# Pairwise 64-row contractions, narrower q and k, and a searched TensorE order in a fused attention + FFN kernel

One core of a Trainium2 chip. The metric is device time in microseconds (us), the median of several runs; a profiled run also gives a span (first to last instruction), which is some 1.7 to 2.1 us shorter than the time.

## The reference, cut to what matters

```python
# S = 2048, D = 448, H = 16 heads of Dh = 28, FF = 1792; weights and x in bf16
xn = layernorm(x)
q, k, v = split(xn @ wqkv)                       # 3 x (S, H, 28)
pq, pk = q @ w_phi, k @ w_phi                    # per head, 28 x 28
phi_q = concat(softmax(pq), softmax(-pq))        # 56 features per head
phi_k = concat(softmax(pk), softmax(-pk))
kv  = phi_k^T @ v ;  z = sum_s phi_k             # per head
o   = (phi_q @ kv) / (phi_q @ z + 1e-6)
out = x + o.reshape(S, D) @ wo + silu(xn @ w1) @ w2
```

The contraction of all projections is 448 = 3.5 x 128. `w_phi` is folded into the q and k weights on the chip ("the fold"), which needs eight DMA transposes of `wqkv`.

Of the kernel before, what the change touches and what calls it, by code (L numbers as in the profile page):

```python
# [107 lines left out]
class _Op:  # L108
    __slots__ = ("id", "eng", "dur", "fn", "deps", "odeps", "table", "name", "start", "end",
                 "ticket", "sigreq", "is_dma", "xfer", "lat", "dma_sem", "dma_val", "users",  # L110
                 "out_slot", "prio", "slack")

    def __init__(self, id, eng, dur, fn, name, table=None):
        self.id = id
        self.eng = eng
        self.dur = dur
        self.fn = fn
        self.deps = set()
        self.odeps = set()
        self.table = table  # L120
        self.name = name
        self.start = None
        self.end = None
        self.ticket = None
        self.sigreq = False
        self.is_dma = False
        self.xfer = 0.0
        self.lat = 1700.0
        self.dma_sem = None
        self.dma_val = None  # L130
        self.users = []
        self.out_slot = None
        self.prio = 0
        self.slack = 0.0


class _Prog:
# [44 lines left out]
    def op(self, eng, dur, fn, reads=(), writes=(), keys_r=(), keys_w=(), table=None, name="",  # L182
           okeys_r=(), okeys_w=()):
        o = _Op(len(self.ops), eng, float(dur), fn, name, table)
        o.prio = self.cur_prio
        o.slack = self.cur_slack
# [17 lines left out]
    def dma(self, fn, xfer, reads=(), writes=(), name="", out_slot=None, eng="sp", issue=450.0, lat=1700.0):  # L204
        o = self.op(eng, issue, fn, reads, writes, name=name)
        o.is_dma = True
        o.xfer = xfer
        o.lat = lat
        o.out_slot = out_slot
        return o  # L210

    def schedule(self):
        ops = self.ops
        n = len(ops)
# [7 lines left out]
        def lat(d, o):  # L222
            if d.is_dma:
                return 0.0
            if d.eng == o.eng:
                return 0.0 if d.eng == "pe" else 60.0
            return 310.0 if d.eng == "act" else 200.0

        bl = [0.0] * n
        for o in reversed(ops):  # L230
            m = 0.0
            for u in o.users:
                uu = ops[u]
                m = max(m, lat(o, uu) + bl[u])
            extra = 2500.0 if o.is_dma else 0.0
            bl[o.id] = o.dur + extra + m
        self.bl = bl
# [6 lines left out]
        eng_free = {e: 0.0 for e in ENGINES}  # L244
        act_table = [None]
        dma_free = [0.0]
# [3 lines left out]
        FILL_TOL = 30.0  # L250

        def est(o):
# [6 lines left out]
            if o.eng == "act" and o.table is not None and act_table[0] is not None and o.table != act_table[0]:  # L259
                t += 1400.0  # L260
            return t

        while done < n:
            cands = []
            tmin = None
            for e in ENGINES:
                for oid in ready[e]:
                    o = ops[oid]
                    t = est(o)
                    cands.append((t, o))  # L270
                    if tmin is None or t < tmin:
                        tmin = t
            assert cands, "scheduler deadlock"
            best = None
            for t, o in cands:
                if t <= tmin + DELTA:
# [5 lines left out]
            for t2, o2 in cands:  # L282
# [8 lines left out]
            if o.is_dma:  # L291
                issue_end = t + o.dur
                xfer_start = max(issue_end, dma_free[0])
                xfer = o.xfer
                dma_free[0] = xfer_start + xfer
                o.end = xfer_start + xfer + o.lat
                eng_free[o.eng] = issue_end
            else:
                o.end = t + o.dur
                eng_free[o.eng] = o.end  # L300
                if o.eng == "act" and o.table is not None:
# [9 lines left out]
        return order  # L311


def bass_parallel_sum__linear_kernel_hedgehog__dense_activation_silu__prompt_kernel(
# [26 lines left out]


# [4 lines left out]
    with es:  # L347
# [13 lines left out]
        Wk = sb("Wk", [128, 4 * D], BF16)  # L361
        Wq_sb = sb("Wq", [128, 4, D], BF16)
        Wk_sb = Wk[:].rearrange("p (k c) -> p k c", k=4)
# [70 lines left out]
        def pe_mms(mms, name, dur=None, keys_w=()):  # L434
# [6 lines left out]
            for _, cnt in mms[0][2].ap[1:]:  # L441
                n *= cnt
            P.op("pe", dur if dur is not None else d_mm(n), fn, reads=[m[1] for m in mms] + [m[2] for m in mms],
                 writes=[m[0] for m in mms], keys_w=keys_w, name=name)
# [4 lines left out]
        def transposes(pairs, name):  # L449
# [5 lines left out]
            P.op("pe", 56.0 * len(pairs), fn, reads=[p[1] for p in pairs] + [ident[:]], writes=[p[0] for p in pairs], name=name)  # L455
# [33 lines left out]
        for i in range(38):  # L489
            P.op("pe", 107.0, lambda e: e.matmul(banks[3][:, 0:128], ones_bf[:], ones_bf[:], start=True, stop=True),  # L490
                 reads=[ones_bf[:]], writes=[banks[3][:, 0:128]], name="warm")
# [9 lines left out]
        def load_x(t0, t1):  # L501
            load(x_sb[:, t0:t1, :], xt[:, t0:t1, :], f"x{t0}")
# [12 lines left out]
        load_w1(0, 512, 3200.0)  # L515
        load_w1(512, 1024, 3200.0)
# [10 lines left out]
        def dma_t(dst, src, xfer, name, **kw):  # L527
            P.dma(lambda e: e.dma_start_transpose(out=dst, in_=src), xfer, lat=650.0, reads=[src] if kw.pop("sbuf", True) else [],
                  writes=[dst], name=name, issue=1250.0, **kw)
# [10 lines left out]
        def fold_loads():  # L540
            for a in range(8):
                dma_t(wT_sb[:, a, :], A_wqkv[:, a * KP:a * KP + 128], 600.0, f"wT_dma{a}", sbuf=False)

        def fold_mms():
            for kt, fb in enumerate((AUX, 2, AUX, 4)):
                for qk in range(2):
                    wps = banks[fb + qk][:, 0:G * KP].rearrange("p (g c) -> p g c", g=G)
                    P.cur_slack = 600.0
                    pe_mms([(wps[:, g, :], wT_sb[0:KP, qk * 4 + g, KS[kt]:KS[kt] + 128], BDphi[:, g, :], True, True) for g in range(G)],
                           "fold", dur=56.0 * G)  # L550
                    P.cur_slack = 0.0
                src = psum[:, fb * 512:(fb + 2) * 512].rearrange("p (b c) -> p b c", b=2)[:, :, 0:D]
                for qk, W in ((0, Wq_sb), (1, Wk_sb)):
                    if qk:
                        copy(W[:, kt, :], src[:, qk, :], 760, "fold_ev")
                    else:
                        act(W[:, kt, :], src[:, qk, :], ACTF.Identity, D, "fold_ev")


        def ln_tile(t):  # L560
# [26 lines left out]
            if t >= XN_DMA0:  # L587
                if t % 2:
                    dma_t(xnT[:, t - 1:t + 1, :, :].rearrange("p i k c -> p (i k) c"),
                          xn_sb[:, sl - 1:sl + 1, :].rearrange("p i c -> p (i c)"), 1300.0, f"xnT_dma{t}")  # L590
# [9 lines left out]

        def pair_block(b0, width, lhs, rhs, name):
            def fulls(st, c0=0, c1=width):
                for i in range(2):
                    for n, kt in enumerate((0, 1, 2 + i)):
                        part = () if (c0, c1) == (0, width) else (c0, c1)
                        mm(banks[b0 + i][:, c0:c1], lhs(i, kt, slice(0, 128)), rhs(i, kt, slice(0, 128), *part),
                           st and n == 0 and c0 == 0, not st and n == 2, name)

            def rem(st):
                rows = [slice(64, 128), slice(0, 64)]  # L610
                return [(banks[b0 + i][:, 0:width], lhs(i, 3 - i, rows[i]), rhs(i, 3 - i, rows[i]), st, not st) for i in range(2)]

            return fulls, rem

        def group(first, rest, name):
            for f in first:
                f[0](True)
            rems = []
            for f in first:
                rems += f[1](False)  # L620
            for f in rest:
                rems += f[1](True)
            pe_mms(rems, name, dur=216.0 * (len(first) + len(rest)) + 214.0)
            for f in first:
                f[2]()
            for f in rest:
                f[0](False)
                f[2]()

        def ffn1_block(fp, c, b0):  # L630
            tok = slice(c * 512, (c + 1) * 512)
            fulls, rem = pair_block(b0, 512, lambda i, kt, r: w1_sb[r, kt, (2 * fp + i) * 128:(2 * fp + i + 1) * 128],
# [6 lines left out]
            return fulls, rem, evac  # L639
# [3 lines left out]
        def v_block(t, b0):  # L643
            fulls, rem = pair_block(b0, D, lambda i, kt, r: xnT[r, t + i, kt, :],
                                    lambda i, kt, r: wv_sb[r, kt, :], "v")
# [6 lines left out]
            return fulls, rem, evac  # L652

        q_order = [14, 15, 4, 5, 6, 7, 0, 1, 8, 9, 2, 3, 10, 11, 12, 13]
# [4 lines left out]

        def proj_block(t, b0, is_k):  # L660
            W = Wk_sb if is_k else Wq_sb
            fulls, rem = pair_block(b0, D, lambda i, kt, r: xnT[r, t + i, kt, :],
                                    lambda i, kt, r: W[r, kt, :], "k" if is_k else "q")

            def evac():
                E2 = ek(t, 2)[:, :, 0:2 * D] if is_k else eq(t, 2)
                src = psum[:, b0 * 512:(b0 + 2) * 512].rearrange("p (i c) -> p i c", i=2)[:, :, 0:D].rearrange("p i (h f) -> p i h f", f=DH)
                dst = E2.rearrange("p i (h s f) -> p i h s f", s=2, f=DH)
                for sg in range(2):
                    act(dst[:, :, :, sg, :], src, ACTF.Exp, 896, "exp", scale=(1.0 if sg == 0 else -1.0), table="exp", okeys_w=["acttab"])  # L670
                E4 = E2.rearrange("p i (h f) -> p i h f", f=DH)
                R2 = Rec[:, int(is_k), t:t + 2, :]
                P.op("dve", 1985, lambda e: e.tensor_reduce(R2, E4, AXL.X, ALU.add), reads=[E4], writes=[R2], name="Ssum")  # L673
                P.op("dve", 555, lambda e: e.reciprocal(R2, R2), reads=[R2], writes=[R2], name="Rrec")  # L674

            return fulls, rem, evac
# [9 lines left out]
        def kv(t):  # L686
            def wide(c):
                return slice(0, 128) if c < CC - 1 else slice(0, KP)

            P.cur_slack = 500.0  # L690
            pe_mms([(banks[KVB][wide(c), c * 2 * DA:(c + 1) * 2 * DA], ek(t)[:, 0, c * KP:c * KP + wide(c).stop],
                     vaug[:, t, 2 * c:2 * c + 2, :].rearrange("p h c -> p (h c)"),
                     t == 0 and c == 0, t == NT - 1) for c in range(CC)], "kv_mm", dur=CC * 32.0, keys_w=["kvbank"])
# [28 lines left out]
        UB = 7  # L722
        ob_cnt = [0]

        def ffn2(t, bs, last):
            w = D // len(bs)
            for ft in range(FT):
                for n, b in enumerate(bs):
                    mm(banks[b][:, 0:w], hT[:, ft, t * 128:(t + 1) * 128], w2_sb[:, ft, n * w:(n + 1) * w],
                       ft == 0, last and ft == FT - 1, "ffn2_mm")  # L730

        def y_tile(t, b):
            P.cur_prio = 2
            ffn2(t, [b], True)
# [6 lines left out]
        u_cnt = [0]  # L741

        def att(t):
            n = u_cnt[0]
            q, uq, oq = n % NQ, n % NU, n % NO
            ub = banks[UB]
            u_cnt[0] += 1
            P.cur_slack = 600.0
# [282 lines left out]
```

## The kernel before: what the change touches

A small scheduler in the kernel lists operations with guessed durations and sets every engine's order. TensorE work comes in blocks of two 128-row output tiles in two PSUM banks: three full 128-row matmuls for each tile, and the half contraction of both as one pair of 64-row matmuls that run side by side in the array.

```python
def pair_block(b0, width, lhs, rhs, name):
    def fulls(st, c0=0, c1=width):
        for i in range(2):
            for n, kt in enumerate((0, 1, 2 + i)):
                mm(banks[b0 + i][:, c0:c1], lhs(i, kt, slice(0, 128)), ...)      # cut
    def rem(st):
        rows = [slice(64, 128), slice(0, 64)]
        return [(banks[b0 + i][:, 0:width], lhs(i, 3 - i, rows[i]), rhs(i, 3 - i, rows[i]), st, not st) for i in range(2)]

def group(first, rest, name):     # the 64-row pairs of 2 to 4 blocks stand together
    ...                           # cut: fulls of `first`, all pairs, fulls of `rest`

# SP's issue order after the loads: input transposes of tiles 4..7, then the weight transposes
chain([f"xnT_dma{t}" for t in (5, 7)] + [f"wT_dma{a}" for a in range(8)] + ["xnT_dma9", "w2"] + ...)
```

TensorE makes FFN1 blocks, v, k, q, the sums kv (58-wide matmuls), U = phi_q kv, and the output tiles. ScalarE empties PSUM (silu, exponentials, v), VectorE does layernorm, softmax sums and final additions, GpSimd scales phi_k and phi_q.

The softmax here doesn't subtract the row's maximum and nothing guards it: scores larger than these inputs give would overflow.

## Time and profile before

| | before |
|---|---|
| time, median of the first runs | 154.15 us (153.79 to 154.19) |
| span of the profiled run | 152.0 us |
| TensorE, first FFN1 matmul to last matmul's end | 6.62 to 149.41 = 142.79 us |
| changes between 128-row and 64-row matmuls | 40, 0.096 us each (median) |
| last matmul's end to end of span | 2.62 us |

The third and fourth lines come from the start times of single matmuls in the trace: the distance from one start to the next, less what the same width takes in an undisturbed run (216 ns for 512 columns, 189 for 448). A busy share alone would not show them. The lines of the profile are in the prediction below.

### The profile page before, as it was taken

Reading aid. Unit: us, or ns where it says so; the run is one execution under the profiler, and the core shown is the slowest. Engines: PE = TensorE matmul, PEld = TensorE weight load, DVE = VectorE, ACT = ScalarE, POOL = GpSimd, SP = SyncE. Lnnn points to the kernel's source line nnn. Section 1 sums busy time; section 2 is a strip of 40 time slices with the busy share of each in tenths; the row PEclk is TensorE's granted clock in tenths of the full one; section 3 lists DMA queues with packets and bytes.
Section 4 is the critical chain, followed back from the end, with each engine's and each line's share of the span. In section 5 each row is a group of like instructions: output and inputs, shape, how many; then the busy total and the mean of one; then the engine's idle time right before and its main releaser. Section 6 shows DMA issues by size and latency. Waiting matters only on the chain.

```text
span 152.0 us, 2799 instructions
## 1 busy us (share of the span) xinstructions
PE 147.6 (97%) x1118; PEld 78.4 (52%) x1118; DVE 89.6 (59%) x171; ACT 72.6 (48%) x86; POOL 67.4 (44%) x76
## 2 busy tenths in 40 slices
PE   7999999999999999999999999999999999999993
PEld 7794434354545555544444544445554555555482
DVE  1958897223048999897105312998953834284552
ACT  3557657393879857895555769774000000000000
POOL 7106455100017999999991000598998000000000
PEclk9999999999999999999999999999999999999999
DMA  4998644499940000000078310075899993534151
GB/s 96 339 370 311 126 89 94 86 237 273 245 129 4 0 0 2 6 0 0 4 138 172 64 40 4 0 136 104 164 118 206 210 195 61 67 102 120 37 157 65
DMA packets 44206, 17.38 MB, mean 114 GB/s; under 512 B 36640, under 2 KB 43808, under 8 KB 44192
## 3 DMA queue, kind: packets, MB, share of 16 engines
q1 hardware_dynamic: 41568, 15.44, 45.1%
q10 hardware_dynamic: 2624, 1.75, 3.9%
q8 instruction: 9, 0.15, 0.5%
q14 instruction: 5, 0.04, 0.1%
HBM read 6.56 MB, written 1.84 MB: 55 GB/s over the span
## 4 chain that ended last, share of the span: by engine, by line
PE 93%; ACT 3%; issue 1%; DVE 1%; POOL 0%; ACTq 0%; POOLq 0%
PE psum L438 90%; PE psum L490 3%; ACT Ek_sb L458 2%; PE psum L453 1%; ACT phT L458 1%; DVE Wk L462 0%; ACT xnT L458 0%; DVE x_sb L776 0%; POOL ones_bf L465 0%; ACTq L971 0%; POOLq L1016 0%
## 5 line engine op out<-in xcount | busy, mean ns | idle before, releaser
L438 PE MATMUL psum<-xnT,phT 128*128 128x512 bf16 (+2 forms) x278 | 48.3, 338 | 0.6 <-ACT xnT L458 0.3
L438 PE MATMUL psum<-w_sb,hT 128*128 128x448 bf16 (+1 forms) x238 | 48.5, 341 | 0.0
L458 ACT ACTIVATE hT<-psum 128x1024 bf16<-128x1024 f32 x28 | 28.1, 1025 | 19.4 <-PE psum L438 19.4
L706 POOL TENSOR_TENSOR RA<-Ek_sb,Rec 128x896 bf16<-128x896 bf16 x16 | 26.6, 1699 | 17.0 <-DVE Rec L674 17.0
L673 DVE TENSOR_REDUCE Rec<-Ek_sb 128x64 f32<-128x1792 bf16 x12 | 23.7, 1990 | 14.1 <-ACT Ek_sb L458 14.1
L438 PEld LDWEIGHTS psum<-w_sb,hT 128*128 128x128 bf16 x238 | 22.3, 98 | 17.5 <-issue 0.6
L438 PEld LDWEIGHTS psum<-xnT,phT 128*128 128x128 bf16 (+1 forms) x278 | 19.8, 98 | 21.6 <-issue 3.6
L458 ACT ACTIVATE Ek_sb<-psum 128x896 bf16<-128x896 f32 x24 | 20.4, 927 | 4.9 <-PE psum L438 3.2
L681 POOL TENSOR_TENSOR Ek_sb<-Ek_sb,Rec 128x896 bf16<-128x896 bf16 x8 | 13.3, 1698 | 4.5 <-ACT Ek_sb L458 4.4
L753 DVE TENSOR_SCALAR den<-psum 128x16 f32<-128x16 f32 x16 | 2.7, 172 | 20.6 <-PE psum L438 20.6
L438 PE MATMUL psum<-wv,xnT 128*128 128x448 bf16 (+1 forms) x64 | 13.4, 352 | 0.1
L438 PE MATMUL psum<-Wk,xnT 128*128 128x448 bf16 (+1 forms) x64 | 13.5, 354 | 0.0
L681 POOL TENSOR_TENSOR phT<-phT,Rec 128x896 bf16<-128x896 bf16 x8 | 13.3, 1698 | 0.0
L438 PE MATMUL psum<-Wq,xnT 128*128 128x448 bf16 (+1 forms) x64 | 12.5, 353 | 0.0
L563 DVE BATCH_NORM_STATS2 st<-x_sb 128x6 f32<-128x448 bf16 x16 | 9.6, 601 | 3.8 <-DMA x_sb<-in_A_x_dram 3.8
L438 PE MATMUL psum<-wo_sb,vaug 128*128 128x448 bf16 (+1 forms) x51 | 11.5, 341 | 0.0
L776 DVE TENSOR_TENSOR x_sb<-psum,x_sb 128x448 bf16<-128x448 f32 (+1 forms) x13 | 7.1, 583 | 6.2 <-PE psum L438 6.2
L578 DVE TENSOR_SCALAR RA<-x_sb,mv,rstd 128x384 bf16<-128x384 bf16 (+2 forms) x28 | 8.8, 349 | 2.7 <-POOL rstd L574 2.6
L760 DVE TENSOR_TENSOR vaug<-psum,rden 128x448 bf16<-128x448 f32 x16 | 9.9, 616 | 0.7 <-DVE rden L755 0.2
L674 DVE RECIPROCAL Rec<-Rec 128x64 f32<-128x64 f32 x16 | 8.6, 540 | 0.3
L673 DVE TENSOR_REDUCE Rec<-phT 128x64 f32<-128x1792 bf16 x4 | 8.0, 1990 | 0.6 <-ACT phT L458 0.6
L458 ACT ACTIVATE phT<-psum 128x896 bf16<-128x896 f32 x8 | 6.9, 930 | 2.9 <-PE psum L438 2.9
(49 smaller groups left out, 113.8 us busy)
## 6 DMA issues: line engine op xcount, KB each, us to landing
out_dram<-x_sb ACTq DMA_DIRECT2D x15, 112.0 KB, 2.4
w_sb<-in_B_w_dram SPq DMA_DIRECT2D x1, 1568.0 KB, 8.1
x_sb<-in_A_x_dram SPq DMA_DIRECT2D x3, 448.0 KB, 7.7
phT<-in_B_w_dram SPq DMA_DIRECT2D x2, 384.0 KB, 4.7
wo_sb<-in_A_wo_dram SPq DMA_DIRECT2D x2, 336.0 KB, 3.9
phT<-in_B_w_dram SPq DMA_DIRECT2D x1, 576.0 KB, 6.9
wv<-in_A_wqkv_dram SPq DMA_DIRECT2D x1, 336.0 KB, 7.3
phT<-in_B_w_dram SPq DMA_DIRECT2D x2, 128.0 KB, 4.6
```

What stands on the lines that cost most here:

```text
L438: r = e.matmul(dst, lhsT, rhs, start=st, stop=sp, skip_group_check=True)
L458: P.op("act", d_act(n), lambda e: e.activation(dst, src, func, scale=scale), reads=[src], writes=[dst], table=table, name=name, **keys)
L490: P.op("pe", 107.0, lambda e: e.matmul(banks[3][:, 0:128], ones_bf[:], ones_bf[:], start=True, stop=True), reads=[ones_bf[:]], writes=[ban ...
L563: P.op("dve", 590, lambda e: e.bn_stats(st6[:, t, :], xs), reads=[xs], writes=[st6[:, t, :]], name=f"bnst{t}", okeys_w=["ln"])
L578: P.op("dve", dur, lambda e: e.tensor_scalar(dst, x_sb[:, t, c0:c1], mv[:, t, 0:1], rstd[:, t:t + 1], ALU.subtract, ALU.mult), reads=[xs, ...
L673: P.op("dve", 1985, lambda e: e.tensor_reduce(R2, E4, AXL.X, ALU.add), reads=[E4], writes=[R2], name="Ssum")
L674: P.op("dve", 555, lambda e: e.reciprocal(R2, R2), reads=[R2], writes=[R2], name="Rrec")
L681: P.op("pool", 1700, lambda e: e.tensor_tensor(E3, E3, Rk[:, :, None].broadcast_to([128, 32, DH]), ALU.mult), reads=[E3, Rk], writes=[E3], ...
L706: P.op("pool", 1700, lambda e: e.tensor_tensor(dst, Eq, Rq.rearrange("p (c j) -> p c j", c=CC)[:, :, :, None].broadcast_to([128, CC, 4, DH ...
L753: P.op("dve", 190, lambda e: e.tensor_scalar(den[:, uq, :], U3[:, :, DH], EPS_DEN, None, ALU.add), reads=[U3[:, :, DH]], writes=[den[:, uq ...
L760: P.op("dve", 620, lambda e: e.tensor_tensor(o3, U3[:, :, 0:DH], rden[:, uq, :, None].broadcast_to([128, H, DH]), ALU.mult), reads=[U3[:, ...
L776: P.op("dve", d_dve(cs.stop - cs.start), lambda e: e.tensor_tensor(res[:, cs], ob, addend[:, cs], ALU.add), reads=[ob, addend[:, cs]], wri ...
```

## The change

Its intent: fewer mode changes, less matrix work, and no waits of TensorE. The core of the diff:

```diff
+            def half(i):            # i = 0 opens the block with 3 pairs, i = 1 closes it with 4
+                lo, hi = i, 1 - i
+                for n, (kl, kh) in enumerate(((0, 0), (1, 1), (2, 3)) if i == 0 else ((0, 0), (1, 1), (2, 2), (3, 3))):
+                    mms.append((banks[b0 + lo][:, 0:width], lhs(lo, kl, LOW), rhs(lo, kl, LOW), st, sp))
+                    mms.append((banks[b0 + hi][:, 0:width], lhs(hi, kh, HIGH), rhs(hi, kh, HIGH), st, sp))
+                ...                 # the closing half waits on TensorE's own semaphore for the opening half
-        Wk = sb("Wk", [128, 4 * D], BF16)                     # 448 columns
-        Wq_sb = sb("Wq", [128, 4, D], BF16)
+        Wqk = sb("Wqk", [128, 2, 4, DQ], BF16)                # DQ = 16 * 27 = 432
+        # the fold subtracts each head's last column from the other 27; the 28th exponential is a constant 1
+        P.op("dve", ..., tensor_tensor(dst, src, ref[...].broadcast_to([128, 2, H, DF]), ALU.subtract), name="fold_sub")
+PLAN = """aF3@4 aF4@0 bF3 aF5@2 av2@6 bF4 bv2 bF5 aF6@0 bF6 av0@4 bv0 aF7@0 aF8@2 aF10@4 bF8 bF10 bF7 f2@26 ...
+ ... W6 W1@2 W10 R3,6,13,1,5,10 F11@1:7 F11:6 F11:1 W11 r11"""    # a/b: open/close a block at a bank; f: fold
-        chain([f"xnT_dma{t}" for t in (5, 7)] + [f"wT_dma{a}" for a in range(8)] + ["xnT_dma9", "w2"] + ...)
+        chain("wT_dma0 wT_dma1 wT_dma2 wT_dma3 xnT_dma5 wT_dma4 xnT_dma7 wT_dma5 wT_dma6 wT_dma7 xnT_dma9 ... w2 ")
```

TensorE follows PLAN strictly; the other engines are still ordered by the scheduler, with new durations. In PLAN the sums kv (K), U and the output tiles (F, W, R) stand wherever the search put them, in any free bank.

## The prediction

> **What bounds the kernel now.** I read the page from the top: busy shares, slices, chain, groups; then the timeline of TensorE around its gaps, and the issue queue of SP. The page first:
>
> ```profile
> span 152.0 us, 2799 instructions
> PE 147.6 (97%) x1118; PEld 78.4 (52%) x1118; DVE 89.6 (59%) x171; ACT 72.6 (48%) x86; POOL 67.4 (44%) x76
> PE   7999999999999999999999999999999999999993
> PEclk9999999999999999999999999999999999999999
> PE 93%; ACT 3%; issue 1%; DVE 1%; POOL 0%; ACTq 0%; POOLq 0%
> L438 PE MATMUL psum<-Wk,xnT 128*128 128x448 bf16 (+1 forms) x64 | 13.5, 354 | 0.0
> ```
>
> TensorE is busy in every slice but the first and the last, at full clock, and is 93% of the chain. So only shorter or better packed TensorE work, or a shorter head or tail, can move the time. "Busy" hides waste, because matmuls overlap: a 448-wide one lasts 354 ns. So I took start-to-start distances of all matmuls instead. In runs of one kind they are constant: 216 ns for 512 columns, 189 for 448, 56 for 128, 29 for the 58-wide ones; two 64-row matmuls on opposite halves of the array start 3 to 5 ns apart, and such a pair takes as long as one full matmul. Everything above these numbers is waste.
>
> The largest waste is the change between 128-row and 64-row matmuls, here before and after the two pairs that end a set of output tiles:
>
> ```profile
> 116.45 0.73 PE L438 MATMUL psum<-wo_sb,vaug 128*128 128x448 bf16 x3
> 117.11 0.55 PE L438 MATMUL psum<-wor_sb,vaug 64*128 64x448 bf16 x4
> 117.59 0.40 PE L438 MATMUL psum<-KVm,phT 112*128 112x58 bf16 x8
> ```
>
> The third 128-row matmul starts at 116.45 + 2 x 0.189 = 116.83, so the first pair was due at 117.02 and starts at 117.11. The second pair starts at 117.31, so the next was due at 117.50 and starts at 117.59. Each change costs about 0.095 us, both ways. The trace has 20 such visits, so 40 changes: 3.8 us. The other gaps are few: 0.29 us at 19.5, 0.27 at 34.8 (a fold bank still being copied), 0.18 at 46.4, small ones early: about 0.9 us from the first projection matmul at 6.62 to the end. The first:
>
> ```profile
> 19.07 1.53 PE L438 MATMUL psum<-xnT,phT 128*128 128x512 bf16 x5
> 19.98 0.34 PEld L438 LDWEIGHTS psum<-xnT,phT 128*128 128x128 bf16 x3 [0.59 <-ACT hT L458]
> ```
>
> The named releaser is an activation, but the transposed input of tiles 6 and 7 landed at 19.87, so I put this wait down to that DMA.
>
> **What the Trainium skill says.** "TensorEngine Tiling (Array Packing)", Key Properties: changing the tiling mode drains TensorE, while tiles run independently; the trace agrees (0.095 us a change, pairs 4 ns apart). The same page, Gotcha 1: different row tiles cannot access one PSUM bank at the same time. The old kernel never tries, so no number here; it is why the new blocks come in two halves. "TensorE: Matmul & The Clock Gate", Back-to-back issue gap: N/2.4 + 2.5 ns warm; the trace agrees (216 at 512, 189 at 448), so 432 should take 182.5. "ScalarE: Activation LUTs", What ACT_TABLE_LOAD costs: about 1283 ns a load; the trace agrees (five of 1283 ns mean).
>
> **Part 1: 64-row contractions throughout.** A block makes two tiles of contraction 448 = 3.5 x 128. Before: six full matmuls and one 64-row pair. After: seven pairs (three opening, four closing, with banks swapped between the halves). The array time is the same, 7 x 216 = 1.51 us for an FFN1 block, 7 x 189 for v. Weight loads double in number, yet two 64-row loads are done within 0.10 us together in the trace, well under a pair's 0.19. What goes is the changes. Walking through the written order word by word (a block half or a remainder is 64-row, all else 128-row) I count 19 changes, plus the one after the head: 20 against 40. **Saved: 20 x 0.095 = 1.9 us**, all on TensorE.
>
> Price: a closing half writes with the lower rows where the upper rows of its opening half wrote, and it waits for TensorE's own semaphore. With another half between them (at least 0.55 us, against 0.38 for a matmul's end) this is free. Twice the order closes a block right after opening it (the seventh FFN1 block and the first v block): there a matmul's 0.38 us plus a semaphore's way stand against 0.22 or 0.19 due. **Added: about 2 x 0.22 = 0.45 us** (an estimate; no such wait is in the old trace).
>
> **Part 2: 432-wide q and k.** The last logit of each head is subtracted in the folded weights, so its exponential is 1. 16 tiles x 2 x 3.5 passes = 112 passes, each 16 columns shorter. 216 - 189 = 27 ns for 64 columns, so 6.7 ns a pass: **0.75 us saved**. 32 exponentials of 864 in place of 896 columns save ACT 0.03 us each. The fold gets two tiny ACT copies per bank pair and a wider DVE subtraction (about 1.05 us: the 0.62 of a 448-wide one plus 416 columns at some 1.04 ns); this matters only for when k can start.
>
> **Part 3: the order, and free placement of kv, U and output tiles.** It can remove at most the 0.9 us of old gaps. Matrix work itself is unchanged. Adding passes from the end of the head (first pair of block 3 at 12.04) at the spacings above, with the 19 changes and the two self-waits, the last matmul starts at 145.4, against 149.15. So with no wait at all TensorE ends 3.75 us earlier.
>
> I then checked, place by place, whether each bank's reader and each operand is ready, with durations of the old trace (silu every 0.91 us, exponentials 0.83, sums 1.99 + 0.54, scaling 1.67 per tile). **What I expect to wait:** (a) the fifth block needs bank 0 at 12.69; the first silu can start at 11.82 and takes 1.02: ready about 12.9, +0.2. (b) Four of the weight transposes now come before the input transposes:
>
> ```profile
> 6.90 0.92 SPq L499 DMA_DIRECT2D x_sb<-in_A_x_dram  x2
> 13.54 3.76 SPq L528 DMA_TRANSPOSE xnT<-RA  x2
> 17.34 11.23 SPq L528 DMA_TRANSPOSE Y_sb<-in_A_wqkv_dram  x8
> ```
>
> SP stood idle from 7.8 to 13.5, and the new order uses that; but those four queue behind input loads that land until 15.7. The second input transpose is then issued at about 18.6 instead of 16.05 and lands about 3.3 us later, near 21.9; TensorE wants it at about 21.4. +0.3, perhaps 0.7. (c) Many later places are within 0.2 us of each other (bank copies in the k/v stretch): +0.3 together. (d) Tail: the last tile is now a whole one: its eviction takes 0.62 instead of 0.39 us, and its store goes through the ACT queue after six others: +0.25.
>
> Sum: -1.9 - 0.75 - 0.9 + 0.45 + 0.2 + 0.3 + 0.3 + 0.25 = -2.05 us. 154.15 - 2.05 = 152.1; I say **152.0**.
>
> **The rivals.** *No waits:* if the search found an order that really keeps TensorE fed, only the tail is lost: -3.75 + 0.25 = -3.5, so 150.6. For it: the old kernel lost only 0.9 us to waits. Against: (a) follows from the trace directly. *GpSimd becomes the bound:* its scaling of k takes 16 x 1.67 = 26.7 us in a row. In the new order it can start near 43.1, so it ends at 69.8, and the last kv product stands at about 71.5 with my waits. A slip of 2 us there, or ones-column fills getting between, would hold TensorE 1 us or so: 153. Against: the slack; k starts some 13 us earlier than before. *The fold comes too early:* its products stand at 26.7 instead of 32.4 and need all eight weight transposes, the last of which lands, by the old latencies (2.6 to 3.9 us), between 25.1 and 26.4. A straggler costs 0.5 to 1 us: 152.5 to 153. *Pairs do not keep their pace over long runs:* the old trace has at most four in a row; 10 ns lost on each of some 310 pairs would be 3 us, and the time would be unchanged. Nothing in the trace suggests it.
>
> **Range and chances.** Better than 2% means under 151.1, so waits, self-waits and tail together must stay about 1 us below my sum; with three terms that I read off the trace I give it 0.22. Being slower by 2% needs over 6 us of new waits: 0.02. The no-wait case and the GpSimd, fold or transpose cases set the ends: 150.5 to 153.3.
>
> **What would show it.** TensorE: 20 changes of 0.09 us; long runs of pairs at 216, 189 and 183 ns; first matmuls of blocks unchanged until 12.0. Gaps of 0.2 at 12.7, of about 0.3 near 21.5, and two of 0.2 at the closing halves near 19 and 20.6. The last matmul should start near 146.5. The prediction is wrong if TensorE waits over 0.5 us before the last kv products, at the fold, or anywhere after 90 us, or if pairs run slower than full matmuls.

## The result

152.19 us (150.91 to 152.60, four runs) against 154.15: ratio 0.9867, 95% interval 0.9824 to 0.9911, 1.3% faster. Ratios here are the mean time of one kernel's fast runs over that of the other's of the same rounds, so not quite the ratio of the medians quoted. Results were correct in all runs, those of the experiments too.

Lines of the page of the changed kernel (the third is TensorE's busy share in 40 slices):

```profile
span 150.8 us, 3406 instructions
PE 144.0 (95%) x1412; PEld 79.1 (52%) x1412; DVE 91.4 (61%) x186; ACT 70.2 (47%) x86; POOL 70.9 (47%) x82
PE   7699968999999999999999999999999999999992
PE 93%; DMA 3%; issue 1%; SPq 1%; DVE 0%
L468 PE MATMUL psum<-Wqk,xnT 64*128 64x432 bf16 x224 | 22.9, 343 | 0.0
```

TensorE is again busy nearly everywhere, but the sixth slice (18.9 to 22.6 us) shows a 6. The chain of waits in order of time (start, us, what) says what the whole run looks like:

```profile
6.67 0.14 issue
6.80 1.21 PE psum L468 x18
...
12.88 0.04 issue
12.92 6.05 PE psum L468 x56
18.97 0.05 issue
19.02 1.62 PE psum L468 x14
20.64 0.05 issue
20.69 0.93 PE psum L468 x8
21.62 1.46 issue
23.08 124.98 PE psum L468 x1196
```

There are four interruptions: at 12.9, 19.0, 20.7 and 21.6 us. From 23.08 to 148.06 TensorE waits for nothing. The last interruption is the large one: 1.46 us without any matmul, and as a start-to-start distance 1.62 us more than due. SP's issue queue in the same run:

```profile
7.33 1.14 SPq L529 DMA_DIRECT2D x_sb<-in_A_x_dram  x2
8.51 7.71 SPq L558 DMA_TRANSPOSE Y_sb<-in_A_wqkv_dram  x4
16.26 1.31 SPq L558 DMA_TRANSPOSE xnT<-RA  x1
17.61 1.27 SPq L558 DMA_TRANSPOSE Y_sb<-in_A_wqkv_dram  x1
18.92 1.31 SPq L558 DMA_TRANSPOSE xnT<-RA  x1
```

The second input transpose (the last line) is issued at 18.92 and lands at 22.99; block 7, which needs tiles 4 to 7, starts at 23.08. In the kernel before, the two transposes of the input were issued at 13.54 and 16.05.

### The profile page after: what moved, and what is told of

Same layout as the page of the kernel before. It is cut to its first block, busy times and chain, and to the rows that moved or that the text cites. A ratio compares the mean times of both kernels' runs of the same rounds, so it can differ in the third digit from the quotient of the medians.

```text
span 150.8 us, 3406 instructions
## 1 busy us (share of the span) xinstructions
PE 144.0 (95%) x1412; PEld 79.1 (52%) x1412; DVE 91.4 (61%) x186; ACT 70.2 (47%) x86; POOL 70.9 (47%) x82
## 4 chain that ended last, share of the span: by engine, by line
PE 93%; DMA 3%; issue 1%; SPq 1%; DVE 0%
PE psum L468 92%; DMA phT<-in_B_w_dram 3%; SPq L529 1%; DVE x_sb L842 0%; PE psum L483 0%
## 5 line engine op out<-in xcount | busy, mean ns | idle before, releaser
L468 PE MATMUL psum<-xnT,phT 64*128 64x512 bf16 (+1 forms) x428 | 45.1, 350 | 2.2 <-issue 1.5
L468 PEld LDWEIGHTS psum<-xnT,phT 64*128 64x128 bf16 (+1 forms) x428 | 21.1, 95 | 22.7 <-issue 1.9
L728 DVE TENSOR_REDUCE Rec<-Ek_sb 128x32 f32<-128x896 bf16 (+1 forms) x20 | 24.3, 1246 | 13.7 <-ACT Ek_sb L488 7.9
L468 PEld LDWEIGHTS psum<-w_sb,hT 128*128 128x128 bf16 x238 | 21.6, 98 | 19.0 <-issue 1.5
L468 PE MATMUL psum<-Wqk,xnT 64*128 64x432 bf16 x224 | 22.9, 343 | 0.0
L488 ACT ACTIVATE Ek_sb<-psum 128x864 bf16<-128x864 f32 x24 | 20.3, 932 | 2.9 <-issue 2.6
L468 PEld LDWEIGHTS psum<-Wqk,xnT 64*128 64x128 bf16 x224 | 10.6, 94 | 9.5 <-ACT Ek_sb L488 0.2
L468 PE MATMUL psum<-wv,xnT 64*128 64x448 bf16 x112 | 12.9, 349 | 0.1
L614 DVE TENSOR_SCALAR RA<-x_sb,mv,rstd 128x384 bf16<-128x384 bf16 (+2 forms) x28 | 10.6, 416 | 1.3 <-POOL rstd L610 1.2
L468 PE MATMUL psum<-wo_sb,vaug 128*128 128x448 bf16 (+2 forms) x51 | 11.0, 341 | 0.0
L842 DVE TENSOR_TENSOR x_sb<-psum,x_sb 128x448 bf16<-128x448 f32 (+2 forms) x14 | 7.6, 585 | 3.8 <-PE psum L468 3.8
L729 DVE RECIPROCAL Rec<-Rec 128x32 f32<-128x32 f32 (+1 forms) x24 | 8.6, 391 | 0.1
```

The lines of the kernel that those rows point to most:

```text
L468: r = e.matmul(dst, lhsT, rhs, start=st, stop=sp, skip_group_check=True)
L488: P.op("act", d_act(n), lambda e: e.activation(dst, src, func, scale=scale), reads=[src], writes=[dst], table=table, name=name, **keys)
L614: P.op("dve", dur, lambda e: e.tensor_scalar(dst, x_sb[:, t, c0:c1], mv[:, t, 0:1], rstd[:, t:t + 1], ALU.subtract, ALU.mult), reads=[xs, ...
L728: P.op("dve", 50 + 967 * n, lambda e: e.tensor_reduce(R2, E4, AXL.X, ALU.add), reads=[E4], writes=[R2], name="Ssum")
L729: P.op("dve", 135 + 210 * n, lambda e: e.reciprocal(R2, R2), reads=[R2], writes=[R2], name="Rrec")
L842: P.op("dve", d_dve(cs.stop - cs.start), lambda e: e.tensor_tensor(res[:, cs], ob, addend[:, cs], ALU.add), reads=[ob, addend[:, cs]], wri ...
```

## The experiments

Twelve kernels ran. Runs that were slow (154.81 of `xnt`, 154.38 of `selfw`, one of 156.22 of the kernel before) are left out of all comparisons of times, and of the medians below. The experiments ran in four groups, each on another chip, and each beside the kernel before: `again`, `xnt`, `selfw` and `xnt_selfw`; the three of section 4 and `unpair`; `again2`, `wide` and `late2_selfw`; `late3`. The unaltered change ran in the first and third group alone, so for the others it is compared by way of the ratios. A yardstick serves throughout: **TensorE's net stretch**, from the start of its first FFN1 matmul to the end of its last matmul, less the wait at block 7. It leaves out the loads at the start, the tail, and that one wait.

### 1. The changed kernel again, twice: `again`, `again2`

> The changed kernel unaltered, to learn how far its single runs spread. If the 1.6 us wait for the second input transpose (profile: TensorE idle from about 21.5 to 23.1) is a matter of when transposes get through, the wait varies between runs: times from 150.9 to 152.7, ratio to the kernel before 0.987 +- 0.004. A rival, noise of TensorE's clock, would show as matmul spacings that differ between profiles; I expect 216, 189 and 183 ns again and only the wait near 21.5 us to differ.

> The changed kernel once more, on the chip and in the rounds of the two runs beside it, as their base: 150.8 to 152.6 us, in two clusters about 1.2 us apart as in the first repeat.

Measured: 151.59 us (150.80 to 152.34), ratio 0.9831, and 151.33 us (150.99 to 152.81), ratio 0.9815; both are "unclear" at the 2% mark. The spans of the first are 149.1, 149.2, 149.4 and 150.3, 150.4, 150.6: two clusters. The second has four of 149.3 to 149.8, one of 150.0 and one of 151.1; the two clusters that were expected there did not come back. The profiles fell in different places of this spread. Here block 7 starts right after the v block, where the profile above had its gap:

```profile
20.08 1.73 PE L468 MATMUL psum<-wv,xnT 64*128 64x448 bf16 x14
21.64 1.67 PE L468 MATMUL psum<-xnT,phT 64*128 64x512 bf16 x14
```

(TensorE's timeline of `again2`: start, us, what.) Three profiles of one program, side by side:

| us | first run | again | again2 |
|---|---|---|---|
| last plain load of x lands | 16.99 | 16.52 | 16.04 |
| fourth weight transpose's issue ends | 16.22 | 15.74 | 15.26 |
| second input transpose lands | 22.99 | 22.48 | 21.51 |
| wait of TensorE at block 7 | 1.62 | 1.13 | 0 |
| first FFN1 matmul starts | 6.80 | 6.84 | 7.00 |
| TensorE's net stretch | 139.63 | 139.56 | 139.59 |
| last matmul's end to end of span | 2.79 | 2.78 | 2.78 |
| span | 150.8 | 150.3 | 149.4 |

The four lines above the span add up to it. TensorE's own work is the same to 0.07 us. What differs is when a load lands, what queues behind it, and the wait that results (and, by 0.2 us, the start). In all three the fourth weight transpose's issue ends 0.77 or 0.78 us before the last load of x lands. "DMA: Bandwidth & Descriptors" in the Trainium skill, Queues, rings and completion order, says that each DMA engine takes descriptors in ring order; the trace agrees: the first weight transpose, issued at 8.51, lands at 17.42, just after the load issued before it (16.99). Why those loads land up to a microsecond apart between runs of one program stays open.

### 2. Another order of the transposes: `xnt`

> Only the order of the issue queue changes: three weight transposes, then the two input transposes, then the other five weight transposes (before: four, one input, one, the second input, three). Theory (the wait is that input transpose, delayed by weight transposes ahead of it): it is issued near 16.1 instead of 18.9 us, lands near 20, the TensorE wait near 21.5 goes from 1.6 to under 0.2 us, and the time falls by 1.0 to 1.6 us against the unaltered kernel, unless the fold (all eight weight transposes, last one landing near 26) then waits; that could give 0.3 us back. Rival (the wait only moves to the fold, since the number of transposes ahead of the fold is the same): the fold waits about 1 us and the time stays within 0.4 us.

```diff
-wT_dma0 wT_dma1 wT_dma2 wT_dma3 xnT_dma5 wT_dma4 xnT_dma7 wT_dma5 ...
+wT_dma0 wT_dma1 wT_dma2 xnT_dma5 xnT_dma7 wT_dma3 wT_dma4 wT_dma5 ...
```

Measured: 151.74 us, ratio 0.9844, against 0.9831 for the unaltered kernel in the same rounds: no gain; the rival was right. The scheduler's guessed durations of the transposes were changed along with their order, here and in sections 4 and 5. The profile fell in a slow run (153.1 us), so its time is not used, but its record names the cause by itself. TensorE's timeline of `xnt`:

```profile
23.77 2.32 PE L468 MATMUL psum<-xnT,phT 64*128 64x512 bf16 x20
28.30 0.95 PE L468 MATMUL psum<-BDphi,Y_sb 112*128 112x112 bf16 x16 [2.21 <-DMA Y_sb<-in_A_wqkv_dram]
```

There is no wait at block 7 any more, and a longer one at the fold, for the weight transposes. `xnt_selfw` (next section) has the same queue order: there TensorE waits 1.33 us at the fold, whose last transpose lands at 27.18.

### 3. The two closing halves moved apart: `selfw`, `xnt_selfw`

> Only TensorE's order changes at one place: open FFN1 block 6, open v block 0, close block 6, close v block 0, in place of open-close, open-close. Theory: the two waits of 0.22 us of TensorE for its own half (18.6 and 20.3 us) vanish. But TensorE then arrives 0.45 us earlier at the input transpose, so it waits 0.45 us longer there: time unchanged (within 0.3 us). Rival (the self-waits cost on their own, whatever follows): 0.45 us faster.

> Both edits. If the input transpose is what hid the self-waits, then now their removal counts: 0.2 to 0.45 us faster than with the queue order alone; about 1.5 to 2 us faster than the unaltered kernel, some 150.3 us in all. If the fold's wait takes over, the two edits together equal the queue edit alone.

```diff
-aF6@0 bF6 av0@4 bv0 aF7@0
+aF6@0 av0@4 bF6 bv0 aF7@0
```

Measured: `selfw` 151.97 us, ratio 0.9858, `xnt_selfw` 152.29 us, ratio 0.9880; neither gains. In `selfw` the two self-waits are gone, and block 7 waits 1.53 us, now with its releaser named:

```profile
20.11 0.92 PE L468 MATMUL psum<-wv,xnT 64*128 64x448 bf16 x8
22.39 0.82 PE L468 MATMUL psum<-xnT,phT 64*128 64x512 bf16 x6 [1.37 <-DMA xnT<-RA]
```

This is the theory's outcome for `selfw`: what is saved ahead of a DMA wait is waited for at it. But where the DMA is in time (`xnt_selfw`, and later `x12_selfw`, `late2_selfw`), there is a new gap of 0.62 us at the same block. TensorE's timeline of `x12_selfw`:

```profile
20.22 0.92 PE L468 MATMUL psum<-wv,xnT 64*128 64x448 bf16 x8
21.59 1.69 PE L468 MATMUL psum<-xnT,phT 64*128 64x512 bf16 x14 [0.45 <-ACT hT L488]
```

I had not foreseen that: block 6 now closes later, so its silu frees bank 0 at 21.45 instead of 21.12, and block 7, which wants bank 0, is due at 20.98 instead of 21.46. By the traces two self-waits of 0.23 us are cheaper than that one of 0.62. The times do not settle it: `xnt_selfw` is 0.5 us slower than `xnt`, but `x12_selfw` 0.5 us faster than `x12`, where VectorE sets the pace a little later in either case (next section).

### 4. Less load ahead of the transposes: `x12`, `x12_selfw`, `x12_selfw_tail`

> Issue queue only: the last 448 KB of x, not needed for another 15 us, are issued after the two input transposes instead of before the first weight transpose; four weight transposes first, then both input transposes, then the other four. Theory: what delays all transposes is the queue of plain loads ahead of them (the first weight transpose, issued at 8.5, lands at 17.4, right after the last x load at 17.0), so taking 1.1 us of load out of the way brings both the second input transpose (22.5 to 23.0) and the last weight transpose (26.5 to 26.7, in the run with the first edit 27 to 28) forward. I expect the input wait of 1.1 to 1.6 us to shrink to 0 to 0.4, no new wait at the fold above 0.3, and 0.8 to 1.5 us less than the unaltered kernel: 150.4 +- 0.5. Rival (transposes are bound by their own rate, about 1.3 us each from issue, so the tenth one is late whatever precedes it): wait moves to the fold again, time within 0.4 us of the unaltered kernel.

> As x12, and the two closing halves moved apart. If x12 removes the input wait, the two 0.22 us waits now count and this is 0.3 to 0.45 us faster than x12, about 150.0. If a transpose still bounds the stretch, no difference.

> As x12_selfw, and the last output tile is made in two banks (320 and 128 columns) as tile 15 already is, so the last eviction is 128 columns wide. I expect the stretch from the last matmul's end to the end of the span to fall from 2.8 to about 2.5 us, and the time by 0.2 to 0.3 us. Rival (the last store waits for the stores before it on the queues): no change.

```diff
+... wT_dma3 xnT_dma5 xnT_dma7 x12 wT_dma4 ...     # x12: the last 448 KB of x, before: ahead of wT_dma0
-F11@1:7 F11:6 F11:1 W11 r11
+F11@17:7 F11:6 F11:1 E11                          # tail only: last tile in two banks, 320 + 128 columns
```

Measured: 152.64, 152.10 and 152.07 us, ratios 0.9921, 0.9875 and 0.9870; none is faster than the unaltered change (0.9831 and 0.9815 on other chips). For the transposes the theory held: the second input transpose lands at 19.70, the wait at block 7 is 0, and the fold starts at 26.47 without a wait (its last transpose landed at 26.04). But TensorE now waits 0.95 us at the second half of the fold. Lines of all engines of `x12`:

```profile
26.47 0.96 PE L468 MATMUL psum<-BDphi,Y_sb 112*128 112x112 bf16 x16
26.88 2.49 DVE L614 TENSOR_SCALAR RA<-x_sb,mv,rstd 128x384 bf16<-128x384 bf16 x2 [0.59 <-POOL rstd L610]
29.29 2.01 DVE L592 TENSOR_TENSOR Wqk<-psum,last 128x864 bf16<-128x864 f32 x2
31.44 0.95 PE L468 MATMUL psum<-BDphi,Y_sb 112*128 112x112 bf16 x16 [0.88 <-DVE Wqk L592]
```

The second half needs the banks of the first, which VectorE empties by the fold's subtraction (L592). VectorE first normalises the last tiles of x (L614), and these now land at 21.59 instead of 16.04 (`again2`); so the subtraction starts at 29.29 instead of 27.70. One of these normalisations takes 2.27 us where others take 0.37. In every profile of a changed kernel just one is that slow (2.26 to 2.36 us; none in the kernel before), and it runs while GpSimd writes its two blocks of constants (26.72 to 29.04 here); in section 5 those writes were moved to 20 us, and the slow one moved with them. So the edit did not merely push the transposes' wait to the fold, as its rival said: it made a third wait, of VectorE. The tail's edit did what it was for (2.62 us from the last matmul's end to the end of the span, 2.77 without it), too little to see in the times.

### 5. The load behind all eight: `late2_selfw`, `late3`

> As selfw, with the last 448 KB of x issued after all eight weight transposes, their tiles normalised later (between and after the fold's subtractions), and v blocks 10 and 14 exchanged since tiles 14 and 15 come later. Theory (input wait and fold wait are one and the same delay: the plain loads plus ten transposes on one queue): with 1.1 us of load gone from ahead of all ten, the last weight transpose lands near 25 instead of 26 to 26.7, neither the input nor the fold waits over 0.4 us, and the time falls by 0.7 to 1.3 us below the unaltered kernel: 150.4 +- 0.6. Against it: later tiles 12 to 15 may make a v block near 42 us wait, which would show as a new gap there.

> late2_selfw, with FFN1 block 8 opened ahead of block 7 (bank 2 is free earlier than bank 0, whose silu now ends later), and the last output tile in two banks (320 and 128 columns). Theory: the 0.62 us gap that appeared near 20.9 in every run with the closing halves moved apart is the wait for block 6's activation in bank 0, so 0.65 us of other work ahead of it removes it; the fold is then wanted at about 25.8 and its last transpose lands near 26.0, so up to 0.3 us comes back there; the tail gives 0.15 us. 0.3 to 0.7 us less than late2_selfw's 151.4: about 150.9. Rival (the fold's transposes bound the stretch, so all of it comes back at the fold): 151.2 to 151.4.

```diff
+... xnT_dma5 xnT_dma7 wT_dma4 wT_dma5 wT_dma6 wT_dma7 x12 xnT_dma9 ...
+   # tiles 12 to 15 normalised between and after the fold's subtractions; v blocks 10 and 14 exchanged;
+   # GpSimd's constant columns written after tile 11's layernorm instead of tile 15's
+aF6@0 av0@4 bF6 bv0 aF8@2 aF7@0 aF10@4            # late3: block 8 opened ahead of block 7
+F11@17:7 F11:6 F11:1 E11                          # late3: last tile in two banks
```

Measured: `late2_selfw` 151.42 us, ratio 0.9826 (five of six runs from 151.24 to 151.44, the sixth 153.15 at a lower granted clock, 0.986); that is no faster than `again2` in the same rounds (0.9815), so the forecast of 150.4 failed. Its last weight transpose landed at 26.05, not near 25. In its profile there is no wait for the input, 0.05 us at the fold and none of VectorE at its second half, but the 0.62 us for bank 0, and 0.19 at 34.2 us, before the first k. `late3` removes the 0.62: **150.89 us (150.51 to 151.51), ratio 0.9787, interval 0.9764 to 0.9811**, the lowest median, 2.1% under the kernel before ("unclear" at the 2% mark). That it beats the unaltered change is not shown: the two did not run on one chip, the intervals overlap (0.9768 to 0.9862 for `again2`), and its net stretch, 139.75, is no shorter than the 139.59 of `again2`. What it may do is avoid the slow runs: its spans are 148.8 to 149.8, those of `again` 149.1 to 150.6. TensorE's timeline and SP's queue of `late3`:

```profile
21.02 4.75 PE L468 MATMUL psum<-xnT,phT 64*128 64x512 bf16 x42
25.98 0.95 PE L468 MATMUL psum<-BDphi,Y_sb 112*128 112x112 bf16 x16 [0.22 <-issue]
```

```profile
15.48 2.70 SPq L558 DMA_TRANSPOSE xnT<-RA  x2
18.23 5.62 SPq L558 DMA_TRANSPOSE Y_sb<-in_A_wqkv_dram  x4
23.89 0.58 SPq L529 DMA_DIRECT2D x_sb<-in_A_x_dram  x1
```

The fold still waits 0.29 us (landing 25.64, start 25.98; the same 0.34 to 0.35 us lie between landing and start in `xnt`, `xnt_selfw` and `late2_selfw`): the transposes, not TensorE, set when the fold can start. So both theories of `late3` held in part: 0.5 us came (by the medians, on two chips), 0.3 came back at the fold.

### 6. The narrower q and k by themselves: `wide`

> The changed kernel with q and k multiplied 448 columns wide again (16 zero columns are padded on; evictions still read 432), the order of all engines otherwise the same. Theory: 112 pairs take 189 instead of 183 ns, 0.75 us in all, and TensorE has no slack behind them: in the profile pair spacings of 189 ns and a last matmul 0.75 us later for the same waits; median 0.5 to 1.0 us above the unaltered kernel. Rival (q and k's stretch waits for GpSimd or ScalarE anyway): under 0.2 us.

```diff
-Wqk = sb("Wqk", [128, 2, 4, DQ], BF16)
+Wqk = sb("Wqk", [128, 2, 4, D], BF16)      # columns 432..447 are zero; evictions still read 432
-fns = pair_block(b0, DQ, ...)
+fns = pair_block(b0, D, ...)
```

Measured: 152.98 us, ratio 0.9906, against 151.33 and 0.9815 for `again2` in the same rounds. That difference (1.4 us by the ratios) is more than the 0.5 to 1.0 expected; it mixes the width with the waits for the input transpose. The trace separates them: pairs 189 ns apart instead of 183, and a net stretch of 140.33 us (wait at block 7: 1.41), 0.74 us over the 139.59 of `again2`. Its group line, to be held against the 22.9 us of the changed kernel:

```profile
L468 PE MATMUL psum<-Wqk,xnT 64*128 64x448 bf16 x224 | 23.7, 349 | 0.0
```

### 7. The pairing undone: `unpair`

> The changed kernel with its new order, but every block made as six full matmuls and one 64-row pair. That makes 104 changes between 128-row and 64-row matmuls instead of 20. Theory (each change costs 0.095 us of TensorE): 84 x 0.095 = 8.0 us more; less the two self-waits (0.45) and most of the input wait (TensorE arrives 1.1 us later there): 6 to 7.5 us slower than the unaltered changed kernel, 157.5 to 159. Rival (pairing brings nothing, the gain is the order's and the narrower q and k's): within 1 us of the unaltered one.

```diff
-   # half(i): 3 or 4 pairs of 64-row matmuls
+   mms = [three full matmuls of tile i] + (rest() if i else [])     # and one pair when the block closes
```

Measured: 159.83 us, ratio 1.0373, 3.7% slower than the kernel before and about 8.2 us slower than the unaltered change (151.59 of `again`, on another chip): more than the 6 to 7.5 expected. The trace has 104 changes of mode: 0.096 us (median) going into a pair, 0.106 coming out. Half of 84 at each makes 8.5 us, more than the 8.0 expected; one of them hides a wait of 0.70 at block 7, which starts at 23.01 when the second input transpose has landed (22.92). Less that wait the net stretch is 147.92, 8.3 us more than with pairs: 8.5 - 0.46 (no self-waits here) - 0.1 (the wait at 12.9 is 0.10 instead of 0.21) = 7.9; the other 0.4 us are spread over many distances, each less than 0.025 us above its width's. The span and busy line show that a share of busy time tells nothing of this; TensorE looks fuller here than in the faster kernel (95%):

```profile
span 158.3 us, 2817 instructions
PE 153.0 (97%) x1118; PEld 76.0 (48%) x1118; DVE 91.6 (58%) x186; ACT 72.0 (45%) x86; POOL 71.0 (45%) x82
```

The last two experiments say that the width is worth what it should be, that pairing is worth somewhat more, and that the new order without pairing would have been a loss. The order by itself (the prediction's part 3) was not tested: no run has the new blocks in the old order, so what it is worth is read from the traces alone.

## Why the prediction was right, point by point

| term of the sum | predicted | measured |
|---|---|---|
| 20 changes of mode fewer | -1.9 | -1.9 (40 and 20 counted, 0.096 each) |
| 432-wide q and k | -0.75 | -0.74 (`wide`) |
| old gaps gone | -0.9 | -1.2: none of the three named is left, nor a fourth of 0.29 |
| self-waits, two | +0.45 | +0.46 (0.23 each, at 18.6 and 20.3) |
| bank 0 not yet emptied at 12.7 | +0.2 | +0.21, in every run but `unpair` (0.10) |
| second input transpose | +0.3, perhaps 0.7 | +1.62, +1.13 or 0 |
| near ties of banks | +0.3 | 0 |
| tail | +0.25 | +0.17 (2.79 against 2.62) |

The mechanism and the total held: 152.0 predicted, 152.19, 151.59 and 151.33 measured. **One wait was mis-sized: that for the second input transpose.** I took 3.3 us from its issue to landing, and an issue at 18.6; it was issued at 18.92, 18.45 and 17.97, and took 4.1, 4.0 and 3.5 us. The old trace had the better number: the same transpose took 3.83 us there (16.05 to 19.88), which with an issue at 18.6 would have given 22.4, a wait of 1.0. The prediction named the queue behind the x loads as the reason, and the three profiles bear that out: as the last load lands 0.5 us earlier at each step, the transpose lands 0.5 and then 1.0 us earlier. What it missed is that this is no fixed wait but one that differs between runs of one program, from 0 to 1.62 us.

**The savings were too small.** The prediction's own two sums do not agree: its terms give TensorE 1.9 + 0.75 + 0.9 - 0.45 = 3.1 us, its walk through all passes 3.75, and it went on with the terms. Measured, at equal starts and without the waits for bank 0 and the input, the last matmul starts 3.5 us earlier. Of what the terms lack, one piece is a fourth old wait, at 66.3 us, where TensorE waits for an exponential; a change of mode falls in the same place, and the prediction counted it as that alone. The chain of the kernel before passes through it:

```profile
63.73 2.57 ACT Ek_sb L458 x3
66.30 0.05 issue
66.34 83.08 PE psum L438 x600
```

That distance is 0.39 us above its width's, four changes' worth. Another 0.3 us was spread over many distances, each at most 0.025 us above its width's. So the central number owes something to luck: a wait larger by 0.8 to 1.3 us (none in `again2`) was balanced by savings larger by 0.4 and by the 0.3 us for near ties, which did not show.

Of the rivals: *no waits* describes the fastest runs (150.80 and 150.91 were measured, 150.6 named), though even the profile without an input wait has the 0.21 at bank 0. *GpSimd becomes the bound* and any wait after 23 us are refuted by the chain of waits, 124.98 us of TensorE in one piece. *Pairs do not keep their pace* is refuted: 216 ns (median of 167) at 512 columns, 189 at 448, 183 at 432. *The fold comes too early* did not happen in the profile of the change itself (its last transpose landed at 26.68, the fold started at 27.72), but it stood right behind: in `xnt` and `xnt_selfw`, where another order of the queue removed the input's wait, the fold's appeared. Input transpose and fold are held up by the same queue of DMAs, which is why reordering the transposes gained nothing, while a plain load moved behind the input transposes took both waits (0 and 0 in `x12`, 0 and 0.29 us in `late3`); in `x12` VectorE's work on that load then came late.

## What to carry to other kernels

When an engine is busy nearly throughout, as TensorE here at 95 to 97%, add up start-to-start distances against the undisturbed spacing of each width: that shows mode changes and small waits which busy time hides. Look into the mode changes too: one of them hid a wait of 0.29 us. A wait at the front of a chain can hide the next one behind it: before moving work or transfers, ask which is the next thing to be late, what the moved piece will then stand in front of, and who needs the moved piece. And where the times of one program spread over more than a microsecond, compare profiles of a slow and a fast run before believing a difference of medians.

## What the Trainium skill lacked or had wrong

- "TensorEngine Tiling (Array Packing)", Key Properties, says that changing the tiling mode drains TensorE but not what it costs: here 0.096 us a change between 128-row and 64-row matmuls (0.106 on leaving a single pair).
- The same page says that different row tiles cannot access one bank at the same time, with no price for keeping to it: closing a block right after opening it, with a wait on TensorE's own semaphore, cost 0.23 us.
- "TensorE: Matmul & The Clock Gate", HAM oscillation, puts the harmful idle gap at more than about 3.4 us. In the profile of `xnt` a wait of 2.2 us was followed by 3.4 us at half clock (29.4 to 32.8 us, granted clock 0.50, pairs 427 instead of 216 ns apart). It is one run; runs of the kernel before also show a mean clock of 0.989 (156.22 and 155.74 us), so that the wait was the cause is not shown.
- "DMA: Bandwidth & Descriptors", DMA Transpose (X-bar), gives no time from issue to landing behind other transfers, nor does another page: here 2.6 to 5.1 us for a transpose issued between 16 and 28 us, and 8.0 to 9.5 us for the first one, issued behind the loads of x; and one and the same transpose landed between 21.5 and 23.0 us in three runs of one program.
